# Five more split products in the first up pass, and a new order of the vector work around them

## The chip, the cores and the metric

The kernel runs on one core of one Trainium2 chip. A core has five engines that run side by side and meet only through semaphores: TensorE (PE in the profile, its weight loads are PEld), VectorE (DVE), ScalarE (ACT), GpSimd (POOL) and SyncE (SP), which issues most of the DMAs. Each engine works through its own list of instructions in order; an instruction that waits holds up all that is behind it on its engine.

The metric is the device time of one execution in microseconds (us); the number given for a kernel is the median of its runs.

## What is computed

One transformer layer without its softmax: a linear-attention block and a gated feed-forward block, each behind a layer norm and each added to its input.

```python
# x: 2048 tokens x 1024, 32 heads of 32; F = 3584
q, k, v = split(layernorm(x) @ wqkv)
phi = lambda t: where(t > 0, t + 1, exp(t)) + 1e-6
kv, z = phi(k)^T v, sum(phi(k))            # per head
h = x + (phi(q) kv / (phi(q) z + 1e-6)) @ wo
n = layernorm(h)
out = h + (relu(n @ W_gate) * (n @ W_up)) @ W_down
```

The change lies in the feed-forward block, in the products with `W_gate` and `W_up` of the first half of the tokens.

## The kernel before

**Planning.** The Python code doesn't issue instructions at once. `PL.add(engine, ...)` appends an operation to its engine's list and derives from the buffers that it reads and writes which earlier operations it must wait for. So the order on each engine is the order in which the Python code calls `PL.add`, and nothing reorders it later. Much of the code therefore passes lists of small functions around ("steps"), and calls them at chosen places.

**Two passes.** The feed-forward block handles the tokens in two passes of 1024 (`p_` or `ps_` is 0 and 1; the text calls them pass 1 and pass 2). Each has an up pass (`ffn_unit`, 14 units) and a down pass (`down_pass`, the product with `W_down`). Units come in pairs: an even unit computes the gate for 512 hidden features, the odd one behind it the up product for the same 512. Both write to `hh`, the hidden activations in SBUF; the odd one multiplies its result in.

**Products.** A unit is a matrix product cut in two in each dimension. The kernel uses the Strassen-Winograd scheme, seven block products P1 to P7 in place of eight. Its operands are sums of blocks: `Ssum` of the activations (once a pass), T1 to T4 of the weights (`t_sums`, VectorE, for each unit; T1 and T3 can be one instruction, T13, or apart when `split` is set). A block product is two halves `u`, each of four matmuls with 512 columns.

Some block products are themselves done by the same scheme one level down, as seven small products, each a quarter of the output: P1 of the next unit (R1 to R7, with sums g1 of the weights), and, in the units listed in `M0`, the fifth product P5 (M1 to M7, with sums g5 of T1 that `w_inner` makes, three VectorE instructions). A small product is two matmuls of 256 columns, so a split P5 is 14 of these and a plain one 8 of 512. In a unit outside `M0`, ScalarE copies P5 from PSUM (s5, twice); in one inside it, ScalarE does M5c, M1c, M6c and M4c and VectorE does s5a.

**PSUM.** Eight banks. Partial results are shared by copying a bank before more is accumulated on it: fk1 (P1 of the next unit, ScalarE, at the end of a unit), fk2 (after P6). P2 of a unit accumulates onto the bank that the fk1 before it has read.

**One unit inside `M0`** runs on TensorE as M1, M5, P2, M6, M2, P6 first half, M7, M3, R1, R5, P6 second half, P7 first half, R2, R6, M4, P7 second half, P3 first half, R7, R3, P3 second half, P4 first half, R4, P4 second half. The results leave PSUM as h11 (copy or relu on ScalarE), c22 (VectorE, after P7), Ra (VectorE, for R), c12 (VectorE, after P3), and h21 (in the next unit, `late21`: a copy h21c on ScalarE and for odd units a product on VectorE). An odd unit ends with h2, a VectorE product over two blocks. h21c writes the buffer of c22, which h2 reads.

**What else VectorE does in pass 1's up pass.** For the down pass's weights: WT1, WT2, WT3 (`wd_pair`, from `wraw`, in even units) and WL (`wl_sums`, in odd ones). Sums of the hidden activations for the down pass: D1 (two feature blocks added) and D3 (two token blocks subtracted), made by `hh_pair` in units 3, 5 and 7 for the pairs 0 to 5 of `hh` (`QD = 6`), the rest in the down pass.

**ScalarE** has the layer norm of the tokens of pass 2 as well: 8 tiles `t`, each in three steps (mean, square, norm), handed to `ffn_unit` as `lna` and `lnb`, two in a unit and three in units listed in `LN3`. `ln_o` is their order. A step's small arithmetic is on GpSimd. The norm step stores its tile to DRAM and loads the tile two further on into `hl`.

**The places that matter** in a unit's Python order: `pre` (ahead of all), `wina`, `winb` (after P6), `mid` (GpSimd's sums), `lna`, `lnb`, `tail` (after c12), `later`, `late21`. In `M0` units of pass 1, `lna` stands behind c22, in others behind the first h11. DMAs go to SyncE in the same order: WT3's stores, the weights of a later unit (`load_w_next`), `load_wraw`, the norm's store.

The lines that a reader of the trace meets: L902 all matmuls, L907 ScalarE's copies, L942 and L1586 the LN steps, L1642 and L1647 T1 to T4 and T13, L1697 g1 (from RWG) and g5 (from RO), L1786 VectorE's c22, c12, h11, h21, h2, Ra and s5a, L1798 the relus h22 and h12, L826 WT, L853 WL, L1663 D1, L1668 D3, L1674 D2, L1996 the down pass's sums, L2060 its evacuations.

Of the kernel before, what the change touches and what calls it, by code (L numbers as in the profile page):

```python
# [132 lines left out]
def bass_sequential_preLN__linear_attn_block__glu_gated_reglu__prompt_kernel(  # L133
# [71 lines left out]
    with es:  # L205
# [1522 lines left out]

        late21 = []

        M0 = (2, 4, 6, 8, 10, 12, 13)
        QD = 6
        LN3 = (11,)

        def inner1(ps_, n):
            return 0 < n < NPAIR
# [1 line left out]
        def ffn_unit(ps_, n, pre, wina, winb, mid=(), lna=(), lnb=(), tail=(), tail2=()):  # L1738
# [23 lines left out]
            def go(fs):  # L1762
                for f_ in fs:
                    f_()
# [35 lines left out]
            def out11(u):  # L1800
                if up:
                    ident_act(c12[:, u, :], bank(BA[u]), [B_bank[BA[u]]], [B_c12[u]], "h11c")
                else:
                    d = H2(0, 0)
                    ident_act(d[0][:, u], bank(BA[u]), [B_bank[BA[u]]], d[1][u:u + 1], "h11", func=ACTF.Relu)
# [66 lines left out]
            def p6(u):  # L1872
                prod(u, BB[u], t_blk(u, 1), s_blk(1), False, "P6")
                fk2(u)
# [14 lines left out]
            if not useM:  # L1889
                if plain:  # L1890
                    p1()
                go(late21)
                late21.clear()
                p5(0)
                p2()
                run(mid, 1)
                out11(0)
                go(lna)
                p5(1)
                go(wina)  # L1900
                p6(0)
                r15()
                p6(1)
                run(mid, 1)
            else:
                sub(cX, B_X, B_(0, 0), A(0, 0), True, "M1")
                sub(cD, B_X, G(0), XS(0), False, "M5")
                ident_act(m5, cD, [B_X], [B_s5[0]], "M5c")
                ident_act(c0, cX, [B_X], [B_0], "M1c")
                go(late21)  # L1910
                late21.clear()
                if n == 0:
                    p1()
                else:
                    p2()
                sub(cX, B_X, G(1), XS(1), False, "M6")
                sub(c0, B_0, B_(1, 0), A(0, 1), False, "M2")
                ident_act(cD, cX, [], [B_X], "M6c")
                if n == 0:
                    p2()  # L1920
                go(wina[:1] if m_first else wina)
                out11(0)
                p6(0)
                sub(cX, B_X, G(2), XS(2), False, "M7")
                sub(cD, B_X, B_(1, 1), XS(3), False, "M3")
                dve(ftmp[:, 1, :].rearrange("p (t c) -> p t c", t=2), bank(BE[1]).rearrange("p (t c) -> p t c", t=2),
                    m5.unsqueeze(1).to_broadcast([P, 2, SHB]), [B_X, B_s5[0]], [B_s5[1]], "s5a")
                go(wina[1:] if m_first else ())
                run(mid, 1)
                r15()  # L1930
                p6(1)
                if nxt and ps_:
                    m4()
# [10 lines left out]
            later.clear()  # L1944
            prod(1, BB[1], t_blk(1, 2), s_blk(2), False, "P7")
            run(mid, 3 if m_first else 1)
            evac5(1, 1, BB, c22, B_c22, "c22")
            if m_first:
                go(lna)
            if up:  # L1950
                d, db = H2(0, 0)
                dve(d, d, c12, B_c12, db, "h11", ALU.mult)
            if not up:
                fin5(1, 1, c22, B_c22, "h22")
            prod(0, BC_[0], w_blk(0, 1, 1), s_blk(3), False, "P3")
# [86 lines left out]
        def down_pass(ps_, fill):  # L2042
# [260 lines left out]
            sg5 = l2_sums(q_d1, sgs[4], "sg5")  # L2303
            if not last:
                claim(B_sgg, B_w[0:4])
                at(0, 4, lambda: d1_sum(QD, NPAIR), lambda: d2_sum(QD, NPAIR))
                at(2, 0, *sg6[0:2])
                at(2, 1, *sg6[2:4])
                at(2, 2, lambda: d3_sum(QD, NPAIR), *sg7[0:2])
                at(2, 3, *sg7[2:4])  # L2310
                at(2, 4, *sg4)
                at(1, 1, lambda: d4(0, NH))
                at(1, 5, lambda: d4(NH, NPAIR))
                for i in range(4):
                    at(3, 2 + i, sg5[i])
            else:
                for i in range(4):
                    at(1, 2 + i, sg7[i])
                claim(B_W, B_hnT)
                sg2 = l2_sums(q_10, sgs[2], "sg2")  # L2320

                D4C = ((0, 4), (4, 7), (7, 11), (11, NPAIR))

                def spread(pi, fs, cs=(3, 4, 5, 6)):
                    for f_, c_ in zip(fs, cs):
                        at(pi, c_, f_)
                spread(0, sg2)
                at(0, 6, lambda: d2_sum(0, NH))
                at(2, 0, lambda: d2_sum(NH, NPAIR))
                spread(2, sg6)  # L2330
                spread(3, sg5, (2, 4, 5, 6))
                for i, c_ in enumerate(((1, 6), (3, 3), (4, 6), (5, 0))):
                    at(*c_, sg4[i])
                for i, c_ in enumerate(((1, 4), (1, 6), (3, 5), (5, 0))):
                    at(*c_, lambda i=i: d4(*D4C[i]))
                at(2, 3, lambda: ld_h(0, 1))
                at(3, 6, *each(add_h, U, 0, 1, order=hi))
# [312 lines left out]
        late_load(0)  # L2650
        late_load(1)
        ln_steps = [late_steps(t) for t in range(TPP)]
        ln_o = [(0, 0), (0, 1), (0, 2), (1, 0)]
        for t in range(1, TPP - 1):
            ln_o += [(t, 1), (t + 1, 0), (t, 2)] if t % 2 else [(t, 1), (t, 2), (t + 1, 0)]
        ln_o += [(TPP - 1, 1), (TPP - 1, 2)]
        ln_q += [(ln_steps[t][i], t if i == 2 else None) for t, i in ln_o]

        early = []
        for p_ in range(NPASS):  # L2660
            done = []
            for q in range(NPAIR):
                pre, wina, winb = [], [], []
                if q == 0:
                    pre += x_inner(p_)
                else:
                    pre.append(tq[1])
                if inner1(p_, q + 1):
                    pre += w_inner1(p_, q + 1)
# [4 lines left out]
                if p_ == 0:  # L2674
# [19 lines left out]
                    if q % 2 == 0:  # L2694
                        wds = wd_pair(q)
                        (tail if q == 0 else wina).extend(wds[0:2])
                        if q == 0 or q not in M0:
                            (winb if q else tail).append(wds[2])
                        wls, raw, nxt_raw, raw_l = wl_sums(q // 2)
                        if q == 0:  # L2700
                            raw = [int, int] + [lambda i=i, r=raw: (r[i](), r[i + 1]()) for i in (0, 2)]
                    else:
                        wina += wls
                        raw = raw_l
                        nxt_raw()
                        if q == NPAIR - 1:
                            for _ in range(2):
                                load_wd_next()
# [7 lines left out]
                        tail += [lambda t=t: early_c(t) for t in range(STB)]  # L2716
                    if q + 1 in M0:
                        tail = w_inner(q + 1) + tail
                    if q and q % 2 == 0 and q in M0:
                        tail.append(wds[2])  # L2720
                    if q + 2 == min(M0):
# [44 lines left out]
                        load_wd_next()  # L2766
            if p_ == 0:
                claim([B_D2], B_S)
                d2_sum(0, QD)
            for f_ in late21:  # L2770
                f_()
            late21.clear()
# [94 lines left out]
```

## Time and profile before

| | us |
|---|---|
| median of 3 runs | 709.62 (709.57 to 709.85) |
| the profiled execution, its own time | 709.65 |
| its span, first to last instruction | 707.9 |
| TensorE busy in the span | 702.4 |
| VectorE busy | 613.9 |
| ScalarE busy | 412.5 |
| GpSimd busy | 182.1 |
| pass 1, units 1 to 13 | 236.48 to 388.11 |
| pass 1, down pass, starts | 388.11 |
| pass 2, units 1 to 13 | 479.35 to 629.79 |
| an even unit of pass 1 / an odd one, 1 to 11 | 11.69 / 11.89 |

The granted TensorE clock was 1.000 over the span. A line of a timeline has the start in us from the beginning of the span, the length, engine, source line, operation, what it writes and reads, shape and count; in square brackets is how long the engine sat idle before it and what ended that. Instructions of one engine overlap a little, so lengths add up to more than the distance of starts; times worked out in the text go by starts. Matmul lengths include the pipeline's drain, and the starts are what counts. Now and then a matmul's record is missing.

### The profile page before, as it was taken

The numbers are of one execution on the slowest core, as the hardware profiler recorded it, in microseconds if no ns is written. First come the engines' busy times: TensorE is split into PE (matmuls) and PEld (weight loads), VectorE is DVE, ScalarE is ACT, GpSimd is POOL, SyncE is SP. The second block draws the span as 40 slices with busy tenths as digits, with TensorE's granted clock in tenths as the row PEclk, the third lists the DMA queues.
The fourth block names the chain that finished last, engine by engine and source line by source line (L and its number), as shares of the span: only waits on it lengthen the run. The fifth ranks groups of instructions, "written<-read, shape, count | busy, mean of one in ns | idle before, by whom it ended". The sixth has DMA issues, their size and how long they took to land.

```text
span 707.9 us, 13556 instructions
## 1 busy us (share of the span) xinstructions
PE 702.4 (99%) x5125; PEld 400.6 (57%) x5125; DVE 613.9 (87%) x982; ACT 412.5 (58%) x752; POOL 182.1 (26%) x246
## 2 busy tenths in 40 slices
PE   8999999999999999999999999999999999999998
PEld 3444444444444555555555478865555555568887
DVE  6988867899898999999889968887889888989996
ACT  4887666764863687788788111146666767651010
POOL 3221100114892244334341020321111111001331
PEclk9999999999999999999999999999999999999999
DMA  9852345114998788979997999998555564369996
GB/s 297 262 124 63 38 124 163 37 31 94 225 233 249 228 262 280 288 220 272 307 269 238 304 281 329 319 239 238 148 142 170 146 176 145 109 238 308 348 284 184
DMA packets 170385, 148.80 MB, mean 210 GB/s; under 512 B 54352, under 2 KB 146896, under 8 KB 170320
## 3 DMA queue, kind: packets, MB, share of 16 engines
q1 hardware_dynamic: 165328, 143.35, 68.0%
q0 software_dynamic: 4032, 3.67, 3.6%
q8 instruction: 40, 0.66, 0.4%
q10 hardware_dynamic: 960, 0.92, 0.4%
q14 instruction: 25, 0.20, 0.1%
HBM read 101.97 MB, written 33.88 MB: 192 GB/s over the span
## 4 chain that ended last, share of the span: by engine, by line
PE 89%; ACT 2%; POOL 1%; DVE 1%; issue 1%; DMA 0%; DVEq 0%; POOLq 0%; SPq 0%; ACTq 0%
PE ps L902 89%; ACT RAB L942 1%; POOL RAB L1444 1%; DVE RXH L1526 1%; ACT RAB L1559 1%; DMA RE<-RE 0%; ACT RXH L942 0%; POOL s L966 0%; DVE RAB L989 0%; DVE rden L1384 0%; ACT ps L907 0%; POOL s L948 0%; POOL s L1543 0%; POOL s L963 0%; ACT RX L982 0%
## 5 line engine op out<-in xcount | busy, mean ns | idle before, releaser
L907 ACT ACTIVATE ps<-ps 128x512 f32<-128x512 f32 (+1 forms) x283 | 141.9, 511 | 184.0 <-PE ps L902 140.4
L902 PE MATMUL ps<-RC,RO 128*128 128x512 f16 (+1 forms) x588 | 138.5, 364 | 0.0
L902 PEld LDWEIGHTS ps<-RC,RO 128*128 128x128 f16 x588 | 57.4, 98 | 45.8
L902 PE MATMUL ps<-RC,RWG 128*128 128x512 f16 x320 | 81.1, 380 | 0.2 <-ACT ps L907 0.2
L907 ACT ACTIVATE RE<-ps 128x512 f32<-128x512 f32 (+3 forms) x106 | 63.5, 613 | 29.5 <-PE ps L902 15.2
L902 PE MATMUL ps<-RH,RWG 128*128 128x512 bf16 (+1 forms) x344 | 76.6, 347 | 0.0
L1786 DVE TENSOR_TENSOR RE<-ps,RE 128x1024 bf16<-128x1024 f32 (+1 forms) x49 | 48.6, 993 | 27.4 <-PE ps L902 26.6
L902 PE MATMUL ps<-RH,RO 128*128 128x512 bf16 (+1 forms) x256 | 65.5, 380 | 0.0
L902 PE MATMUL ps<-RW,RAB 128*128 128x256 f16 (+3 forms) x358 | 52.8, 300 | 0.0
L902 PEld LDWEIGHTS ps<-RH,RWG 128*128 128x128 bf16 x344 | 33.1, 98 | 32.4
L902 PE MATMUL ps<-RAB 128*128 128x512 bf16 (+3 forms) x242 | 51.2, 349 | 0.0
L2069 POOL DMA_DIRECT2D out_dram<-RX x20 | 17.9, 1292 | 127.3 <-DVE RX L2060 86.5
L902 PEld LDWEIGHTS ps<-RC,RWG 128*128 128x128 bf16 (+1 forms) x320 | 30.0, 98 | 33.7 <-ACT ps L907 5.1
L804 POOL TENSOR_TENSOR RW<-RW 128x256 f16<-128x256 bf16 x28 | 18.9, 675 | 113.0 <-PE ps L902 70.3
L902 PEld LDWEIGHTS ps<-RW,RAB 128*128 128x128 f16 (+1 forms) x358 | 34.9, 98 | 14.2 <-DVE RXH L1480 0.5
L2060 DVE TENSOR_TENSOR RE<-ps,RE 128x512 f32<-128x512 f32 x46 | 31.6, 687 | 11.4 <-PE ps L902 11.0
L1798 ACT ACTIVATE RAB<-RAB 128x1024 bf16<-128x1024 bf16 x28 | 29.5, 1052 | 16.1 <-DVE RAB L1786 16.1
L902 PEld LDWEIGHTS ps<-RH,RO 128*128 128x128 f16 (+1 forms) x256 | 24.4, 98 | 24.4 <-ACT RX L907 1.5
L1786 DVE TENSOR_TENSOR RAB<-ps,RE 128x1024 bf16<-128x1024 f32 x28 | 34.3, 1223 | 3.8 <-PE ps L902 3.7
L907 ACT ACTIVATE RAB<-ps 128x512 bf16<-128x512 f32 (+2 forms) x55 | 35.9, 654 | 2.0 <-PE ps L902 2.0
L1642 DVE TENSOR_TENSOR RO<-RWG,RO 128x1024 f16<-128x1024 bf16 x54 | 37.0, 685 | 0.0
L1786 DVE TENSOR_TENSOR RAB<-RAB,RE 128x1024 bf16<-128x1024 bf16 (+1 forms) x43 | 36.3, 846 | 0.7
(221 smaller groups left out, 1377.2 us busy)
## 6 DMA issues: line engine op xcount, KB each, us to landing
RWG<-in_B_W_gate_dram SPq DMA_DIRECT2D x28, 512.0 KB, 5.7
RWG<-in_B_W_up_dram SPq DMA_DIRECT2D x28, 512.0 KB, 5.4
RW<-l_scr SPq DMA_DIRECT2D x21, 448.0 KB, 4.9
RE<-l_scr SPq DMA_DIRECT2D x17, 448.0 KB, 4.2
RW<-in_B_W_down_dram SPq DMA_DIRECT2D x14, 512.0 KB, 6.4
l_scr<-RX SPq DMA_DIRECT2D x7, 1024.0 KB, 7.0
RW<-t_scr SPq DMA_DIRECT2D x13, 448.0 KB, 5.8
RE<-in_A_x_dram SPq DMA_DIRECT2D x19, 256.0 KB, 3.6
```

Source lines behind the costliest of these rows:

```text
L804: PL.add("pool", lambda e: e.tensor_tensor(out=ly[:, j, :], in0=x[0], in1=y[0], op=ALU.subtract), deps=[PL.prog["pe"][-1]], reads=x[1] + y ...
L902: lambda e: e.matmul(out_ap, lhsT, rhs, start=start, stop=stop, skip_group_check=skip),
L907: PL.add("act", lambda e: e.activation(out=dst, in_=src, func=func), reads=reads, writes=writes, name=name)
L942: PL.add("act", lambda e: e.activation(out=junk[:, c0:c1], in_=src[:, c0:c1], func=func, scale=scale, accum_out=sv[:, col:col + 1]), reads ...
L1444: PL.add(eng, lambda e: e.tensor_tensor(out=s(i)[0], in0=x[0], in1=y[0], op=op), reads=x[1] + y[1], writes=[B_So[z][i]], name="So%d_%d" % ...
L1526: PL.add("dve", lambda e: e.tensor_tensor(out=hsb[:, hs, :], in0=ps[:, b:b + 2, :], in1=x2(st).rearrange("p (a c) -> p a c", a=2), op=ALU. ...
L1559: PL.add("act", lambda e: e.activation(out=xo[:, kx, :], in_=hsb[:, hs, :], func=ACTF.Identity, bias=s2[:, ks, 4:5], scale=s2[:, ks, 2:3]) ...
L1642: PL.add(eng, lambda e: e.tensor_tensor(out=tb(j)[0](r), in0=x[0](r), in1=y[0](r), op=ALU.subtract), reads=rd, writes=bt(j, r), name="T%d_ ...
L1786: PL.add("dve", lambda e: e.tensor_tensor(out=dst, in0=in0, in1=in1, op=op), reads=reads, writes=writes, name=name)
L1798: PL.add("act", lambda e: e.activation(out=d, in_=d, func=ACTF.Relu), reads=[], writes=db, name=name)
L2060: PL.add(eng, lambda e: e.tensor_tensor(out=dst, in0=in0, in1=in1, op=op), reads=reads, writes=writes, name=name)
L2069: PL.add("pool", lambda e: e.dma_start(dst, src, accum_op=ALU.add), reads=[bsrc], writes=[B_hscr[st]], slot=sl, name="acc_%d_%d" % (st, dh))
```

## The change

- `M0` becomes all units from 2 on: the units 3, 5, 7, 9 and 11 of pass 1 get the split fifth product too. With it they get g5 sums for themselves (in the tail of the even unit before), T1 and T3 apart for the unit behind them, `lna` behind c22, and one idle place at the head of `mid`.
- `QD` becomes 0: `hh_pair` isn't called in pass 1 any more. D1 and D3 of the pairs 0 to 5 are made in its down pass: D1 at the start, ahead of D2, and D3 ahead of the rest of D3.
- In the even units 2 to 12 (`T2E`), T2 of the unit moves from its own `pre` to the tail of the odd unit before, ahead of h2; the odd unit's h21 (copy and product) moves from behind M1c to behind the first h11, and so behind WT1.
- In units that aren't `M0` units of pass 1, so in all of pass 2, h11 stands ahead of c22 on VectorE instead of behind it.
- The LN steps come in a new order, and the unit with three of them is unit 1 instead of 11.

```diff
-        M0 = (2, 4, 6, 8, 10, 12, 13)
-        QD = 6
-        LN3 = (11,)
+        M0 = tuple(range(2, NPAIR))
+        QD = 0
+        QE = 6
+        LN3 = (1,)
+        T2E = (2, 4, 6, 8, 10, 12)
...
                 ident_act(c0, cX, [B_X], [B_0], "M1c")
-                go(late21)
-                late21.clear()
+                if not (m_first and n in T2E):
+                    go(late21)
+                    late21.clear()
...
                 out11(0)
+                go(late21)
+                late21.clear()
                 p6(0)
...
             run(mid, 3 if m_first else 1)
+            h11 = []
+            if up:
+                d11, db11 = H2(0, 0)
+                h11.append(lambda: dve(d11, d11, c12, B_c12, db11, "h11", ALU.mult))
+            if not m_first:
+                go(h11)
             evac5(1, 1, BB, c22, B_c22, "c22")
             if m_first:
                 go(lna)
-            if up:
-                d, db = H2(0, 0)
-                dve(d, d, c12, B_c12, db, "h11", ALU.mult)
+                go(h11)
...
-                at(0, 4, lambda: d1_sum(QD, NPAIR), lambda: d2_sum(QD, NPAIR))
+                at(0, 4, lambda: d1_sum(QE, NPAIR), lambda: d2_sum(QE, NPAIR))
...
-                at(2, 2, lambda: d3_sum(QD, NPAIR), *sg7[0:2])
+                at(2, 2, lambda: d3_sum(QD, QE), lambda: d3_sum(QE, NPAIR), *sg7[0:2])
...
-        ln_o = [(0, 0), (0, 1), (0, 2), (1, 0)]
-        for t in range(1, TPP - 1):
-            ln_o += [(t, 1), (t + 1, 0), (t, 2)] if t % 2 else [(t, 1), (t, 2), (t + 1, 0)]
-        ln_o += [(TPP - 1, 1), (TPP - 1, 2)]
+        ln_o = [(0, 0), (0, 1), (1, 0), (0, 2), (1, 1), (1, 2), (2, 0), (2, 1), (3, 0), (2, 2), (3, 1), (3, 2), (4, 0),
+                (4, 1), (5, 0), (4, 2), (5, 1), (5, 2), (6, 0), (6, 1), (7, 0), (6, 2), (7, 1), (7, 2)]
...
-                else:
+                elif p_ or q not in T2E:
                     pre.append(tq[1])
...
-                        raw = raw_l
+                        raw = [int] * (q in M0) + raw_l
...
+                    if q + 1 in T2E:
+                        tail.append(tq[1])
...
-                d2_sum(0, QD)
+                d1_sum(QD, QE)
+                d2_sum(0, QE)
```

## The prediction

> **What bounds the kernel now.** I read the page's busy shares first, then the chain that ended last in order of time, then busy time by stretches (one stretch per unit of pass 1's up pass), then VectorE's, ScalarE's and SyncE's timelines inside two units.
>
> ```profile
> PE 702.4 (99%) x5125; PEld 400.6 (57%) x5125; DVE 613.9 (87%) x982; ACT 412.5 (58%) x752; POOL 182.1 (26%) x246
> ```
>
> ```profile
> 207.52 474.52 PE ps L902 x3025
> 682.04 0.00 issue
> 682.04 23.10 PE ps L902 x210
> ```
>
> TensorE is the bound: from 207.52 to 705.14 us the chain is its matmuls and nothing else. By their starts, a 512-wide matmul is followed by the next after 0.216 us and a 256-wide one after 0.109, and from 222 us on only three gaps exceed this, 0.13 to 0.17 us each. So removed matmuls are worth their full time, and no wait stands there to be removed. What can go wrong is a new wait.
>
> ```profile
> 248.37:260.06 11.69, 11.69 (x70) 6.59 (x69) 11.10 (x19) 10.20 (x19) 5.71 (x7) 1.00 0.91 292
> 260.06:271.94 11.88, 11.88 (x63) 6.06 (x62) 10.89 (x17) 9.05 (x18) 6.98 (x7) 1.00 0.86 271
> 271.94:283.63 11.69, 11.69 (x69) 6.59 (x68) 11.12 (x19) 10.20 (x19) 4.13 (x6) 1.00 0.76 238
> 330.79:342.68 11.89, 11.89 (x64) 6.06 (x62) 9.61 (x15) 9.06 (x18) 5.66 (x7) 1.00 0.90 242
> ```
>
> These are units 2, 3, 4 and 9 (columns: length, then busy time of PE, PEld, DVE, ACT, POOL). An even unit, with its fifth product split, takes 11.69 us, an odd one 11.89. VectorE is idle 0.6 us in an even unit, 1.0 in unit 3 and 2.3 in unit 9: it is the second bound.
>
> ```profile
> 268.11 1.22 DVE L1786 TENSOR_TENSOR RE<-ps,RE 128x1024 bf16<-128x1024 f32 x1 [0.79 <-PE ps L902]
> 270.45 1.21 DVE L1786 TENSOR_TENSOR RE<-ps,RE 128x1024 bf16<-128x1024 f32 x1
> 271.58 0.44 DVE L1697 TENSOR_TENSOR RE<-RO 128x512 f16<-128x512 f16 x1
> 272.05 0.62 DVE L1697 TENSOR_TENSOR RE<-RO,RE 128x256 f16<-128x256 f16 x2
> 272.59 1.22 DVE L1786 TENSOR_TENSOR RAB<-RAB,RE 128x2048 bf16<-128x2048 bf16 x1
> 273.72 0.68 DVE L1642 TENSOR_TENSOR RO<-RWG,RO 128x1024 f16<-128x1024 bf16 x1
> ...
> 277.12 0.68 DVE L1786 TENSOR_TENSOR RE<-ps,RE 128x512 f32<-128x512 f32 x1
> ...
> 278.92 0.69 DVE L1642 TENSOR_TENSOR RO<-RWG 128x1024 f16<-128x1024 bf16 x1
> 279.78 1.23 DVE L1786 TENSOR_TENSOR RAB<-ps,RE 128x1024 bf16<-128x1024 f32 x1 [0.18 <-PE ps L902]
> ```
>
> VectorE from the end of unit 3 through unit 4: c22 of the odd unit, c12, the three g5 sums, h2, T2, later s5a, T1, then c22 of the even unit. Between the first c22 and the last it never idles; its spare time is 0.79 us ahead of the odd unit's c22 (2.11 in unit 9) and 0.18 ahead of the even one's. A 1024-wide sum holds it 0.60 us from start to start.
>
> **The products.** Each of units 3, 5, 7, 9, 11 loses eight 512-wide matmuls and gains fourteen 256-wide ones: 8 x 0.216 = 1.73 against 14 x 0.109 = 1.53. The stretches say the same: 11.887 - 11.690 = 0.197. Times five: **-0.985 us**.
>
> The Trainium skill, "TensorE: Matmul & The Clock Gate", Back-to-back issue gap, speaks against this: in a stream of weight loads and matmuls it has one matmul per 81 ns at 128 columns and per 131 ns at 512. A line through these gives, as an estimate, 98 ns at 256, and 14 x 98 against 8 x 131 would make each unit 0.32 us longer, 711.2 us in all. The trace disagrees, with 216 ns at 512 columns.
>
> **VectorE's new work in an odd unit.** g5 for it (three sums, 271.58 to 272.59: 1.01), s5a (0.60), and T1 and T3 apart for the next unit (2 x 0.60, for one T13 of 1.14): +1.67. Units 3, 5, 7 lose a D1 and a D3 sum (two 1024-wide, 262.31 to 263.64: 1.33). Net +0.34 there and +1.67 in 9 and 11, in units 0.20 shorter, against idle pairs of 1.57 and 2.86 us. It fits in sum, with about 1 us left per pair; where the pieces stand decides.
>
> *Odd unit.* g5 now stands ahead of T3 and WT3 in the even unit's tail, so T2 of the odd unit ends 2.3 us after the unit's start and its P6 begins at 2.60: hidden. VectorE reaches c22 about 0.9 us before P7 is over: hidden. ScalarE takes M5c, M1c, M6c, M4c for two s5 copies, and the LN step that stood behind h11 now stands behind c22 with the other; the queue then ends about 10.9 us into the unit, and fk1 waits for c12 until 11.4: hidden by 0.5.
>
> *Even unit.* From the odd c22 on nothing is idle, so the one sum that is new in this stretch, T3, makes all behind it 0.60 late. T2 ahead of h2 keeps T2 early (it ends 1.9 us into the unit; P6 begins at 2.60; unmoved and with T3 ahead it would end at 3.1). h21c, behind h2 in ScalarE's queue, now also stands behind M6c and h11; fk2, queued behind it, ends 4.9 us into the unit and P7 begins at 5.19: hidden by 0.2 after the hand-over. Two waits open:
> - s5a ended at 277.80, M4 (same bank) began at 278.44. It will end at 278.40; VectorE's end to the matmul it releases is 0.05 to the weight load and 0.05 more (g5 ends 272.02, load 272.07; load 272.33, matmul 272.38). M4 is 0.06 late.
> - c22 starts 0.34 late (0.60 less the idle time). h22, one LN step and fk1 follow it on ScalarE without a gap; fk1 ended at 283.73 and will end at 284.07, so P2 of the odd unit starts at 284.17 and not at 283.63 + 0.44. 0.10 late, the 0.06 included.
> Four pairs (4/5 to 10/11) at 0.10 and unit 12 at 0.06 (no LN step stands in its queue): **+0.45**. Ends: 0 if the chain is 0.1 shorter, and 1.35 if each pair pays 0.3, half of the added 0.60.
>
> **SyncE.** WT3 ends 1.0 us later in the odd unit, and its stores, two weight loads and the next wraw loads are queued behind it. Weights are needed a unit later. wraw is closer: it landed 3.6, 3.5 and 2.9 us before WT1 needed it in units 4, 6, 8, but 1.0 in unit 10 (345.72 against 346.71; a transposing load of 1.86 us stands in that queue) and 1.7 in unit 12. With 1.0 later stores and a unit 0.2 shorter, WT1 of unit 10 waits about 0.2: **+0.2**, all of which the chain passes on. Ends: 0 and 0.5. In unit 2, where no T3 is new, WT1 starts 0.6 earlier (h21 now follows it), just as its wraw lands (251.79): 0, s5a there has 0.6 to spare.
>
> **The LN steps.** Norms 1, 3, 5 move a unit earlier, with their stores and the loads of hl; each load is still issued at least a unit before its mean step (loads land in 2.6 to 7.7 us). The third step of unit 1 is 1.14 us in 2.1 us of ScalarE's idle time: 0. GpSimd does the same sums and is idle 4 us and more per unit. Without that cover a step costs its excess once.
>
> **The sums in the down pass.** D1 and D3 of pairs 0 to 5 are two 3072-wide sums of 1.75 (the D2 of that size, 389.26), 3.5 to 3.6 us with gaps.
>
> ```profile
> 410.59 1.09 DVE L1996 TENSOR_TENSOR RWG<-RAB,RWG 128x1792 f16<-128x1792 bf16 x1
> 415.61 1.42 DVE L2060 TENSOR_TENSOR RE<-ps,RE 128x512 f32<-128x512 f32 x2 [3.93 <-PE ps L902]
> ```
>
> VectorE idles 3.93 us there, after the last of the sums that follow; D2 and sg6 end near 402.6 and TensorE reads them from 412.28 on. 0. With that cover gone, the first evacuation would be late by the excess, and its bank is next written near 434: still 0.
>
> **h11 ahead of c22** (pass 2; unit 1 of pass 1). In pass 2 c22 idles 0.14 ahead of itself at 510.58; with h11 (0.60) in front it starts 0.4 later and ends at about 9.45 us into the unit, and P4, which needs it, begins at 9.75: hidden by 0.2. 0; ends 0 and 7 x 0.1.
>
> **Sum.** -0.985 + 0.45 + 0.2 = -0.33 on the profiled execution's own 709.65 us (span 707.9 and 1.7 around it), 0.03 over the median, 709.62: **709.3**.
>
> **Rivals.**
> - *No new wait* (the chain 0.1 shorter, wraw in time): 709.65 - 0.985 = 708.6. For it: all margins are near zero, not far below. Chance 0.25.
> - *Waits use up the gain*: 0.3 per pair, 1.35, and 0.5 for wraw: 710.2; from 709.7 to 711.0. Against it: idle time of 1 us per pair remains. 0.16.
> - *Slower*: ScalarE's queue in odd units. Both LN steps now stand between M4c and fk1 with 0.5 us to spare. If a step waits there (GpSimd's lsum sum of 1.15 us can stand ahead of a rstd), all beyond 0.5 delays P2 of the next unit. It passes 711.0 from about 0.9 us of waiting in each of five units; at 1.15 it is 709.3 + 5 x 0.65 = 712.5. Against it: each norm follows its square step by half a unit or more. 0.13.
> - *Narrow matmuls don't pay*: if the 0.098 us weight load did not hide beside a 256-wide matmul, spacing would be 0.207, and five units 5 x (14 x 0.207 - 1.73) = +5.8: 715.5. The even units' 11.69 speak against it. The Trainium skill's rule named above belongs here. 0.02.
> - *Faster by more*: all five savings and the three present gaps (0.46): 708.2. Nothing in the change touches those. 0.03.
>
> **How the numbers follow.** My forecast has 0.41 (709.0 to 709.7). The range 708.4 to 710.6 takes in no wait, the forecast and most of the used-up gain, 0.8 in all. 0.2% is 1.4 us, about what a measurement of this kernel can tell from no change: slower 0.13 + 0.02, faster 0.03, within 0.82.
>
> **What would show it.** Odd units 3 to 11 of 70 matmuls and 11.69 to 11.8 us; gaps of some 0.05 us ahead of M4 in units 4 to 12 and ahead of the first P2 in 5 to 11; WT1 of unit 10 waiting for wraw; VectorE's idle time ahead of the first down-pass evacuation down from 3.93 to about 0.3. It is wrong if fk1 in odd units waits for an LN step, if a unit is above 11.89, or if pass 2's units leave 11.69.

## The result

The changed kernel takes 713.32 us, the median of 6 runs (712.38 to 713.96), against 709.82 (709.57 to 710.04) for 6 runs of the kernel before. The ratio is 1.0047, with a 95% interval of 1.0034 to 1.0060: half a per cent slower, and 2.7 us above the range that was forecast. The profiled execution, the slowest of the six, took 713.96 us, with a span of 712.2.

### The profile after

From the page of the changed kernel, the busy times and the chain that ended last, by engine:

```profile
PE 703.0 (99%) x5155; PEld 404.3 (57%) x5155; DVE 623.8 (88%) x1003; ACT 414.1 (58%) x762; POOL 177.8 (25%) x246
...
PE 76%; DVE 9%; DMA 3%; ACT 2%; issue 2%; POOL 1%; SPq 1%; DVEq 0%; POOLq 0%; ACTq 0%
```

TensorE's busy time hardly moves, but the chain is no longer its own: TensorE has 76% of it, against 89% on the page of the kernel before, and VectorE 9% against 1%. Busy time by units of pass 1 (units 2, 3, 4, 8, 9; columns: length, then busy time of PE, PEld, DVE, ACT, POOL):

```profile
249.38:261.74 12.36, 11.86 (x69) 6.57 (x68) 11.28 (x18) 9.70 (x19) 6.60 (x8) 1.00 0.88 276
261.74:273.43 11.69, 11.69 (x69) 6.66 (x68) 10.55 (x18) 9.82 (x19) 4.84 (x6) 1.00 0.79 235
273.43:285.61 12.18, 11.86 (x69) 6.54 (x68) 11.94 (x20) 9.69 (x20) 5.23 (x9) 1.00 0.81 267
...
321.18:333.98 12.80, 12.04 (x69) 6.50 (x68) 12.56 (x20) 9.87 (x19) 4.70 (x7) 1.00 0.93 269
333.98:345.67 11.69, 11.69 (x69) 6.64 (x68) 10.55 (x18) 9.82 (x19) 4.83 (x6) 1.00 0.79 210
```

The odd units took the whole saving: 11.89 to 11.69 each. The even units pay: 11.69 became 12.36, 12.18, 12.19, 12.80, 12.41 and 12.18 in units 2 to 12, 3.99 us in sum. Units 2 to 12 together took 129.58 us before and take 132.58 now. The rest of the 4.3 us between the two spans is 1.01 us ahead of unit 1 and 0.23 in one unit of pass 2. The stretch from the start of pass 1's down pass to unit 1 of pass 2 has its 91.24 us as before.

In the even units TensorE waits at one place, M4 (and in unit 8 at M5 too). TensorE in unit 4 (timeline; R6 is `ps<-RX,RAB`, M4 is `ps<-RC,RE`; in brackets the wait that the profile sees):

```profile
279.71 0.38 PE L902 MATMUL ps<-RX,RAB 128*128 128x256 f16 x2
280.41 0.39 PE L902 MATMUL ps<-RC,RE 128*128 128x256 f16 x2 [0.32 <-DVE RE L1788]
```

Two 256-wide matmuls after 279.71, M4 was due at 279.93; it came 0.48 later, behind s5a. What VectorE and GpSimd did just before, in two timelines of the changed kernel (L1788 is what was L1786; WT1, h21, s5a; and GpSimd's first WM sum of the unit, which a matmul releases):

```profile
277.46 1.23 DVE L826 TENSOR_TENSOR RW<-RW 128x2048 f16<-128x2048 bf16 x1
278.60 1.16 DVE L1788 TENSOR_TENSOR RAB<-RAB,RE 128x1024 bf16<-128x1024 bf16 x1
279.68 0.68 DVE L1788 TENSOR_TENSOR RE<-ps,RE 128x512 f32<-128x512 f32 x1
```

```profile
277.64 1.57 POOL L879 TENSOR_TENSOR RAB<-RW 128x256 f16<-128x256 bf16 x1 [4.00 <-PE ps L902]
```

h21 takes 1.16 us; in the kernel before, where it stood ahead of WT1, the same product took 0.69 (h21, WT1):

```profile
275.38 0.69 DVE L1786 TENSOR_TENSOR RAB<-RAB,RE 128x1024 bf16<-128x1024 bf16 x1
275.98 1.22 DVE L826 TENSOR_TENSOR RW<-RW 128x2048 f16<-128x2048 bf16 x1
```

And GpSimd's sum takes 1.57 where its like takes 0.67 (at 283.39 of this profile). The two fit together: the sum came while WT1 ran and ended 0.52 after WT1's end (279.21 against 278.69), and h21 ended 0.55 after the sum. Both are a little under what each needs by itself (0.67, and 0.60 from start to start). So first WT1 holds the sum up, and then the sum, next in turn, holds h21 up. In the kernel before the same sum was stretched in the same way (here its line), but what VectorE ran after WT1 was s5a, which has one input in PSUM, and that took 0.68 as ever:

```profile
276.15 1.58 POOL L879 TENSOR_TENSOR RAB<-RW 128x256 f16<-128x256 bf16 x1 [4.04 <-issue]
```

The Trainium skill, "SBUF — State Buffer", Who interferes with whom, states the rule that this follows: a VectorE instruction with both inputs in SBUF and a GpSimd instruction that reads SBUF share one read interface, whichever comes first holds it for its whole instruction, and the other blocks; a VectorE instruction with at most one SBUF input, outside the modes that use both ports, does not contend. The rows above agree, with 0.48 us as the price here. The part on the cores has the engines meet only through semaphores; here two of them meet without one, since h21 waits for no semaphore of GpSimd and is held all the same.

Two more places of the same kind. In unit 8, GpSimd's 128x512 sum WL starts behind three small LN instructions, and VectorE's first sum of g5, which takes 0.42 elsewhere, takes 1.04; M5 is 0.50 late. GpSimd first, then VectorE:

```profile
319.24 0.19 POOL L963 TENSOR_TENSOR s<-s 128x1 f32<-128x1 f32 x1 [0.71 <-ACT RE L942]
319.51 0.57 POOL L966 TENSOR_TENSOR s<-s,neghalf 128x1 f32<-128x1 f32 x1
320.18 0.27 POOL L1581 TENSOR_SCALAR s<-s 128x1 f32<-128x1 f32 x1
320.40 1.15 POOL L869 TENSOR_TENSOR RX<-RW,RX 128x512 f16<-128x512 f16 x1
```

```profile
319.67 1.22 DVE L1788 TENSOR_TENSOR RE<-ps,RE 128x1024 bf16<-128x1024 f32 x1
320.80 1.04 DVE L1697 TENSOR_TENSOR RE<-RO 128x512 f16<-128x512 f16 x1
```

In units 2 and 10, last, WT1 waits for wraw (VectorE's timeline, the wait in brackets); in unit 10 it then takes 1.45 in place of 1.23, since a WM sum has begun at 349.88:

```profile
253.58 1.23 DVE L826 TENSOR_TENSOR RW<-RW 128x2048 f16<-128x2048 bf16 x1 [0.87 <-DMA RW<-in_B_W_down_dram]
254.72 1.16 DVE L1788 TENSOR_TENSOR RAB<-RAB,RE 128x1024 bf16<-128x1024 bf16 x1
...
350.18 1.45 DVE L826 TENSOR_TENSOR RW<-RW 128x2048 f16<-128x2048 bf16 x1 [0.42 <-DMA RW<-in_B_W_down_dram]
```

### The profile page after: what moved, and what is told of

The parts are those of the page before. It is cut to its first block, busy times and chain, and to the rows that moved or that the text cites. A ratio compares the mean times of both kernels' runs of the same rounds, so it can differ in the third digit from the quotient of the medians.

```text
span 712.2 us, 13655 instructions
## 1 busy us (share of the span) xinstructions
PE 703.0 (99%) x5155; PEld 404.3 (57%) x5155; DVE 623.8 (88%) x1003; ACT 414.1 (58%) x762; POOL 177.8 (25%) x246
## 4 chain that ended last, share of the span: by engine, by line
PE 76%; DVE 9%; DMA 3%; ACT 2%; issue 2%; POOL 1%; SPq 1%; DVEq 0%; POOLq 0%; ACTq 0%
PE ps L902 76%; DVE RAB L1788 2%; DMA RW<-in_B_W_down_dram 2%; DVE RE L1788 2%; DVE RW L826 2%; ACT RAB L942 1%; SPq L653 1%; DVE RO L1642 1%; DVE RE L1697 1%; POOL RAB L1444 1%; DMA r_scr<-RW 1%; DVE RXH L1526 1%; ACT RAB L1559 1%; DMA RE<-RE 0%; DVE RAB L1697 0%
## 5 line engine op out<-in xcount | busy, mean ns | idle before, releaser
L907 ACT ACTIVATE ps<-ps 128x512 f32<-128x512 f32 (+1 forms) x293 | 144.9, 505 | 182.7 <-PE ps L902 147.7
L902 PE MATMUL ps<-RC,RO 128*128 128x512 f16 (+1 forms) x568 | 132.1, 360 | 0.0
L902 PEld LDWEIGHTS ps<-RC,RO 128*128 128x128 f16 x568 | 55.6, 98 | 41.2 <-ACT ps L907 1.0
L1788 DVE TENSOR_TENSOR RE<-ps,RE 128x1024 bf16<-128x1024 f32 (+1 forms) x54 | 52.1, 964 | 25.2 <-PE ps L902 25.2
L1788 DVE TENSOR_TENSOR RAB<-RAB,RE 128x1024 bf16<-128x1024 bf16 (+1 forms) x43 | 38.7, 901 | 0.7
L902 PE MATMUL ps<-RE 128*32 128x33 bf16 (+1 forms) x668 | 35.4, 203 | 0.3 <-DVE RE L1697 0.3
```

The lines of the kernel that those rows point to most:

```text
L902: lambda e: e.matmul(out_ap, lhsT, rhs, start=start, stop=stop, skip_group_check=skip),
L907: PL.add("act", lambda e: e.activation(out=dst, in_=src, func=func), reads=reads, writes=writes, name=name)
L1788: PL.add("dve", lambda e: e.tensor_tensor(out=dst, in0=in0, in1=in1, op=op), reads=reads, writes=writes, name=name)
```

## The experiments

Theory A: GpSimd's sums hold up VectorE's sums that read SBUF twice, above all h21 behind WT1; that is what costs. Theory B: h21 is slow by its place or its operands, or VectorE simply has too much to do. Theory C: ScalarE's queue is too long with the new products (the slower rival of the prediction).

The table puts all profiles side by side: units 2 to 12 of pass 1 in sum, the start of unit 1, and the profiled execution's own time less that start. 128.59 is eleven times 11.69, the whole saving.

| kernel | units 2-12 | unit 1 at | time less start | median of runs | ratio (95%) |
|---|---|---|---|---|---|
| before | 129.58 | 236.48 | 473.17 | 709.82 | |
| changed | 132.58 | 237.49 | 476.47 | 713.32 | 1.0047 (1.0034 to 1.0060) |
| e1 WM behind P7 | 130.03 | 236.26 | 473.72 | 710.32 | 1.0012 (1.0002 to 1.0021) |
| e2 h21 behind s5a | 129.16 | 237.11 | 473.01 | 710.26 | 1.0007 (0.9998 to 1.0017) |
| e3 old units | 129.58 | 236.34 | 473.53 | 709.87 | 1.0005 (0.9996 to 1.0015) |
| e4 h11 back | 132.27 | 237.00 | 476.18 | 712.35 | 1.0040 (1.0025 to 1.0055) |
| e5 e2, old LN order | 130.07 | 236.79 | 473.69 | 710.48 | 1.0010 (1.0001 to 1.0019) |
| e6 products alone | 132.27 | 236.59 | 475.86 | 712.81 | 1.0038 (1.0024 to 1.0051) |
| e7 e5, WY later | 130.07 | 236.07 | 473.78 | 710.87 | 1.0013 (1.0004 to 1.0021) |
| e8 WM twice | 131.70 | 236.54 | 475.36 | 711.90 (one run) | |
| e9 e2, LN steps swapped | 128.59 | 235.97 | 472.43 | 709.37 | 0.9995 (0.9987 to 1.0004) |
| e10 e9, WY later | 128.59 | 237.70 | 472.29 | 709.83 | 0.9998 (0.9985 to 1.0012) |
| e11 as e9 | 128.59 | 236.11 | 472.45 | 709.85 | 1.0002 (0.9993 to 1.0011) |
| e12 as before | 129.58 | 236.23 | 473.18 | 709.41 (one run) | |

The kernel before had medians of 709.50 to 709.68 beside e1 to e12.

### e1: GpSimd's first WM sum behind P7

```diff
                             raw = [int, int] + [lambda i=i, r=raw: (r[i](), r[i + 1]()) for i in (0, 2)]
+                        else:
+                            raw = [int] + raw
```

> In the even units of pass 1 GpSimd's first raw sum of W (WM) is moved behind product P7 and the others follow it, so that none is queued behind WT1. Theory A (the two engines stand in each other's way): h21 takes 0.68 us again in units 4, 6, 8 and 12 (1.16 in the changed kernel), s5a ends 0.47 earlier there, M4 waits under 0.1 us in units 4, 6 and 12 (0.48 in the changed kernel); units 2 and 10, where WT1 waits for a DMA, keep a part of their 0.66 and 0.71. The time falls by some 4 x 0.45 = 1.8 us from 713.3, to 711.5; less if the moved sums are in the way of another VectorE sum. Theory B (h21 is slow by its place or its operands, whatever GpSimd does): h21 still takes 1.16 us, M4 is still 0.48 late, 713.3. Theory C (ScalarE's queue is too long with the new products): M4 is late as before, and the wait is put down to ScalarE; 713.3.

h21 takes 0.68 in every even unit, and M4 of units 2, 4, 6 and 12 waits for less than 0.05 us. VectorE in unit 4, in the same order as in the changed kernel:

```profile
275.56 1.23 DVE L826 TENSOR_TENSOR RW<-RW 128x2048 f16<-128x2048 bf16 x1
276.70 0.68 DVE L1788 TENSOR_TENSOR RAB<-RAB,RE 128x1024 bf16<-128x1024 bf16 x1
277.30 0.68 DVE L1788 TENSOR_TENSOR RE<-ps,RE 128x512 f32<-128x512 f32 x1
```

Nothing on VectorE or ScalarE was changed, so B and C fall for this wait. The up pass is 2.55 us shorter than in the changed kernel, more than the 1.8 expected, since unit 2 gains all of its 0.67. What stays: M5 and M4 of unit 8 (0.51 and 0.13), 0.10 in units 5 and 11, where the moved sums now stretch a sum of g5 from 0.29 to 0.64, and M4 of unit 10, 0.49 late with h21 at 0.68: there WT1 waits 0.41 for wraw (a load that scatters, as told below).

### e2: h21 behind s5a

```diff
-                go(late21)
+                l21 = list(late21)
                 late21.clear()
+                for f_ in l21:
+                    f_(0)          # the copy h21c
                 p6(0)
...
+                for f_ in l21:
+                    f_(1)          # the product h21
                 go(wina[1:] if m_first else ())
```

> VectorE's product h21 is moved behind the sum s5a in the even units of pass 1 (its copy on ScalarE stays where it is), all else as in the changed kernel. Theory A: after WT1 comes s5a, which reads PSUM; GpSimd's first WM sum runs beside it, as before the change, h21 takes 0.68 us, s5a ends 1.16 us earlier than in the changed kernel, M4 waits for nothing in units 4, 6, 8 and 12; 713.3 - 4 x 0.48 = 711.4, or lower where units 2 and 10 gain too (WT1's end 0.7 us earlier than needed): 710.5. What comes behind s5a is 0.68 later than without h21, so M7's and c22's readers could wait. Theory B: s5a is early too, so M4 doesn't tell; but h21 still takes 1.16 us in its new place, or s5a is the one that gets long. Theory C: M4 still late, behind ScalarE.

The other way out: GpSimd stays, VectorE gives way. By the up pass it is the better one (129.16 against 130.03 in e1); the medians, 710.26 and 710.32, don't tell the two apart. GpSimd's sum and VectorE's WT1, s5a and h21 in unit 4:

```profile
276.58 1.58 POOL L879 TENSOR_TENSOR RAB<-RW 128x256 f16<-128x256 bf16 x1 [4.00 <-PE ps L902]
```

```profile
276.40 1.23 DVE L826 TENSOR_TENSOR RW<-RW 128x2048 f16<-128x2048 bf16 x1
277.55 0.68 DVE L1788 TENSOR_TENSOR RE<-ps,RE 128x512 f32<-128x512 f32 x1
278.15 0.68 DVE L1788 TENSOR_TENSOR RAB<-RAB,RE 128x1024 bf16<-128x1024 bf16 x1
```

The same stretched sum now lies under s5a, which reads PSUM and isn't held; h21 has its 0.68 back. s5a writes SBUF as h21 does, so it is what they read that makes the difference. No M4 waits in any unit. In pass 1 only M5 of unit 8 is left (0.51), with 0.06 behind it. So the product that the change put behind WT1 was harmless one place further on.

### e3: the old units, all else as in the changed kernel

```diff
-        M0 = tuple(range(2, NPAIR))
+        M0 = (2, 4, 6, 8, 10, 12, 13)
```

> Units 3, 5, 7, 9, 11 lose the inner fifth product again (8 matmuls 512 wide instead of 14 of 256); the places of h21, T2, the D sums and the LN steps stay as in the changed kernel. The matmuls cost 5 x 0.197 = 0.985 us more again. Theory A: GpSimd still holds up h21 (1.16 us in even units), but VectorE is some 0.6 us earlier in the even unit without T3's sums, so M4 is at most 0.1 late: 713.3 + 0.985 - 3.9 + 0.3 = 710.7. Theory C (the new order is what costs, the products nothing): the stalls stay at 0.48 a unit, 714.2. If h21 takes 0.68 here, the new products are what puts it beside the GpSimd sum.

h21 is held up here too, 1.16 in all six even units from 2 on (VectorE in unit 4):

```profile
275.07 1.23 DVE L826 TENSOR_TENSOR RW<-RW 128x2048 f16<-128x2048 bf16 x1
276.21 1.16 DVE L1788 TENSOR_TENSOR RAB<-RAB,RE 128x1024 bf16<-128x1024 bf16 x1
277.30 0.68 DVE L1788 TENSOR_TENSOR RE<-ps,RE 128x512 f32<-128x512 f32 x1
```

But without T3's sum s5a ends at 277.98, 6.18 into the unit, and M4 is due at 6.50: no unit waits, and all have the lengths of the kernel before. The new order costs nothing that shows by itself (0.25 us in the medians, with an interval that holds 1); the collision is paid for only where the products have used up the slack. It came out 0.8 under the expectation, which had left 0.3 of stalls and the late start in.

### e4: h11 behind c22 again

```diff
-            if not m_first:
-                go(h11)
             evac5(1, 1, BB, c22, B_c22, "c22")
             if m_first:
                 go(lna)
-                go(h11)
+            go(h11)
```

> In pass 2 the product h11 goes behind the evacuation c22 again, all else as in the changed kernel. If h11 ahead of c22 is what makes P4 wait 0.22 us in one unit of pass 2, that gap goes and the time is 713.1; if GpSimd's sum beside WX1 and T4 is the cause alone, the gap shrinks by less than that but goes as well, since c22 is then 0.5 us earlier. Pass 1 is as in the changed kernel (even units 12.18 us, h21 1.16 us). The start of unit 1, 1.0 us later in the changed kernel's profile than in the kernel before, differs between these runs if it belongs to the start-up's transfers, and is 1.0 us late in all four if it belongs to the change.

A miss: the wait of P4 in pass 2 stays (0.22), so h11's place doesn't make it. In that unit c22 is late because GpSimd's sums of Y stand beside T4 and WX1. In the changed kernel T4 takes 1.00 where it takes 0.71 in the kernel before, and WX1 takes 0.90 where it takes 0.42 in other units, having come just after a GpSimd sum began at 596.40. VectorE:

```profile
596.45 0.90 DVE L775 TENSOR_TENSOR RW<-RW 128x512 f16<-128x512 bf16 x1
597.27 1.21 DVE L1788 TENSOR_TENSOR RAB<-ps,RE 128x1024 bf16<-128x1024 f32 x1
```

The first of these GpSimd sums starts 4.2 us into the unit in the profiles of before, e1 and e3, where P4 doesn't wait, and at 4.5 in those of the changed kernel, e2 and e4, where it does. What moves it stays open. The expectations of e7 and e10 call it a load's landing, but no run shows that: in all of these profiles GpSimd's wait ahead of the sum, for TensorE and a transfer, ends 4.11 us into the unit, and the store that the sum itself waits for has landed before the unit begins. The start of unit 1 differs among the four runs, 236.26 to 237.11: it isn't a fixed 1.0 us late.

### e5: e2 with the LN steps in the old order

```diff
-        LN3 = (1,)
+        LN3 = (11,)
...
-        ln_o = [(0, 0), (0, 1), (1, 0), (0, 2), ...
+        ln_o = [(0, 0), (0, 1), (0, 2), (1, 0)]
+        for t in range(1, TPP - 1):
+            ln_o += [(t, 1), (t + 1, 0), (t, 2)] if t % 2 else [(t, 1), (t, 2), (t + 1, 0)]
+        ln_o += [(TPP - 1, 1), (TPP - 1, 2)]
```

> h21 behind s5a as in e2, and the LayerNorm steps back in the old order (ln_o as before the change, LN3 = (11,)). In e2 the up pass of pass 1 loses only 0.51 us, all of it ahead of M5 of unit 8, where VectorE's first sum of g5 takes 1.05 us instead of 0.42 while GpSimd runs a 128x512 sum (WL) that starts behind three small LN instructions. Theory A: with the old order GpSimd is not behind that sum at that moment, g5 takes 0.42, the gap goes, units 3 to 12 are all 11.69 us, the up pass is 0.985 us shorter than before the change and the time is 709.6 - 0.98 = 708.6 (708.9 where pass 2's P4 waits 0.22 us again). Rival: the gap in unit 8 has nothing to do with the LN order (the T5 chain of that unit is simply late): it stays at 0.51, 709.1. Second rival: the old order's steps fall onto another sum and a gap opens elsewhere.

The second rival. M5 of unit 8 is in time, but now M5 of units 4 and 10 is 0.50 late, each behind a g5 sum of 1.04 beside the same WL sum, and P2 of unit 12 waits 0.34 for fk1 (three LN steps stand in unit 11's ScalarE queue in this order). GpSimd at the end of unit 3:

```profile
270.13 0.20 POOL L963 TENSOR_TENSOR s<-s 128x1 f32<-128x1 f32 x1 [0.71 <-ACT RE L942]
270.40 0.56 POOL L966 TENSOR_TENSOR s<-s,neghalf 128x1 f32<-128x1 f32 x1
271.06 0.27 POOL L1581 TENSOR_SCALAR s<-s 128x1 f32<-128x1 f32 x1
271.29 1.15 POOL L869 TENSOR_TENSOR RX<-RW,RX 128x512 f16<-128x512 f16 x1
```

The pattern is that of unit 7 in the changed kernel. In the old order units 3 and 9 have a square step (t, 1) as their first LN step, in the new one unit 7 alone. So the LN order isn't free, and by the up pass (130.07 against 129.16 in e2) the change's new order is the better of the two; the medians, 710.48 and 710.26, don't show it.

### e6: the products alone, in the kernel before

```diff
-        M0 = (2, 4, 6, 8, 10, 12, 13)
+        M0 = tuple(range(2, NPAIR))
```

> The kernel before with the inner fifth product in units 3, 5, 7, 9, 11 too, and nothing else of the change (h21 at its old place ahead of WT1, D sums in the up pass, old LN order). Theory A: h21 is not behind WT1, so GpSimd's sum runs under s5a as before and h21 takes 0.68; M4 is at most 0.1 late. VectorE has 1.56 us idle per pair of units before, the products ask for 1.67 more, so in the units that keep a D pair (3, 5, 7) it runs 0.1 to 0.7 us late by the end: stalls of 0.1 to 0.5 us in units 4 to 8, none later. The time is 709.6 - 0.98 + 0.3 to 1.5 = 708.9 to 710.1. Rival (VectorE's lateness is what the products cost, wherever h21 stands): even units lose 0.48 or more each, 711.5 to 713.

Here the rival's time came true, 711.5 to 713, and theory A's 708.9 to 710.1 was a miss. h21, ahead of WT1, takes 0.69, and M4 is never late, as A has it. But units 4 to 12 still lose 0.50 to 0.76 in every even one. In units 4 to 10 most of it is at P6, which starts 0.49 to 0.54 late behind T2; in unit 12 the larger part is P2, 0.34 behind fk1 as in e5. VectorE's h2 and T2, then TensorE, in unit 4:

```profile
273.46 1.22 DVE L1786 TENSOR_TENSOR RAB<-RAB,RE 128x2048 bf16<-128x2048 bf16 x1
274.60 0.68 DVE L1642 TENSOR_TENSOR RO<-RWG,RO 128x1024 f16<-128x1024 bf16 x1
```

```profile
274.58 0.38 PE L902 MATMUL ps<-RC,RO 128*128 128x256 f16 x2
275.34 0.60 PE L902 MATMUL ps<-RC,RO 128*128 128x512 f16 x2 [0.37 <-DVE RO L1642]
```

This is the wait that T2 ahead of h2 removes. So the products need a new order on VectorE, the change has it, and one step of it, h21 behind WT1, gives the gain back by another door.

### e7 and e10: the last sums of Y one product later

```diff
-                    wys = [f_ for m in range(NM) for f_ in y_wsums(m) + [int]]
+                    wys = [f_ for m in range(NM) for f_ in ([int] + y_wsums(m) if m == 6 else y_wsums(m) + [int])]
```

> As e5, and in pass 2 GpSimd's last group of sums of Y starts one product later, so that its first one no longer falls beside T4 and WX1 in unit 10. Theory A: P4 of that unit waits for nothing, whatever the load's landing; 708.6, and 0.2 less than e5 wherever e5's profile has that gap. Rival: the gap comes back at another product of the same or the next unit, since VectorE's sums with two SBUF inputs stand everywhere there; same as e5.

> As e9, with the last group of Y's sums of pass 2 on GpSimd one product later (as in e7). Theory A: up pass as in e9; unit 10 of pass 2 is 11.69 us whatever the landing of its load, 708.6. Rival: no gain over e9, since that wait comes in some executions only, or a new wait in units 10 and 11 of pass 2.

P4 of pass 2 waits in neither (e9 and e11, without this, have it: their unit takes 11.92, so 0.23 is lost in each; the 0.45 in the expectation of e11 is the distance over a missing matmul record). In e5, though, it is gone as well, and in the medians nothing shows. Inconclusive as a gain.

### e8: the WM sum twice

```diff
-            raw = [lambda: addw(0, wr(0, 1), wr(0, 0)),
+            raw = [lambda: [addw(0, wr(0, 1), wr(0, 0)) for _ in range(2 if m else 1)],
```

> The changed kernel with GpSimd's first WM sum of each even unit from 2 on issued twice (the same values are written again), so that two GpSimd sums of 0.67 us stand in a row behind WT1. If GpSimd and VectorE take turns, h21 gets in behind the first one: it takes 1.16 us as in the changed kernel, M4 waits 0.48, and the second sum ends late. If GpSimd keeps the port while it has work, h21 takes 1.16 + 0.67 = 1.83 us and M4 waits 1.15. If GpSimd has nothing to do with it, M4 waits 0.48 and neither sum is stretched.

They take turns. M4 of units 4, 6, 10 and 12 waits 0.48 to 0.49, as that of 4, 6 and 12 does in the changed kernel; the two GpSimd sums, VectorE's WT1 and h21 in unit 4:

```profile
276.01 2.65 POOL L879 TENSOR_TENSOR RAB<-RW 128x256 f16<-128x256 bf16 x2 [4.00 <-PE ps L902]
```

```profile
275.84 1.23 DVE L826 TENSOR_TENSOR RW<-RW 128x2048 f16<-128x2048 bf16 x1
276.98 1.16 DVE L1788 TENSOR_TENSOR RAB<-RAB,RE 128x1024 bf16<-128x1024 bf16 x1
```

The second sum, issued at 277.67, took 0.99 and ended at 278.66, 0.52 after h21: GpSimd's second sum waited for h21, not h21 for it. In this run h21 is held by one GpSimd sum and not by two.

### e9 and e11: e2 with two LN steps swapped

```diff
-                (4, 1), (5, 0), (4, 2), (5, 1), (5, 2), (6, 0), (6, 1), (7, 0), (6, 2), (7, 1), (7, 2)]
+                (5, 0), (4, 1), (4, 2), (5, 1), (5, 2), (6, 0), (6, 1), (7, 0), (6, 2), (7, 1), (7, 2)]
```

> As e2 (h21 behind s5a), and in the new LN order the two steps of unit 7 change places: (5, 0) first, (4, 1) second. In the changed kernel and in e2 unit 7 is the only odd unit whose first LN step is a second one (t, 1), and the only one with a slow g5; in e5 those were units 3 and 9, and the slow g5 stood there: a step (t, 1) in the first place of an odd unit puts three small GpSimd instructions ahead of the 128x512 sum WL, which then runs beside g5. Theory A: with the swap no odd unit has it, g5 takes 0.42 us everywhere, M5 of unit 8 waits for nothing, units 2 to 12 are all 11.69 us, and pass 1's up pass is 0.985 us shorter than before the change: 709.6 - 0.98 = 708.6, 0.23 more where P4 of pass 2 waits. Rival: the step falls onto another sum in its new place; a gap of 0.3 to 0.5 us stays in unit 7 or 8, 709.1.

> The kernel of e9, unchanged, once more. Its first profile had units 2 to 12 all at 11.69 us and a span of 706.7, 1.2 under the kernel before, and yet its median was only 0.13 lower. If the rest is lost ahead of pass 1 (unit 1 has begun between 235.97 and 237.70 us in the profiles so far, of kernels whose code is the same up to there), units 2 to 12 are 11.69 us again, whatever the time, and the time less the start of unit 1 is that of the first profile, but for up to 0.45 of pass 2's P4. If it is lost in the up pass (wraw's landing, another sum beside GpSimd's), a unit longer than 11.69 us shows it.

> The kernel before, once more, for a second profile of it. Unit 1 began at 236.48 us in the first. If that start scatters over 1.7 us in any kernel, another value is likely here and the time moves with it; if it is steadier without the new products, it stays within some 0.2 us of 236.48 and the time within 0.2 of 709.65.

In the up pass of pass 1 theory A holds to the last wait. Busy time in units 2, 3, 4, 8 and 9 of e9:

```profile
247.86:259.55 11.69, 11.64 (x69) 6.64 (x68) 10.96 (x18) 9.90 (x19) 5.70 (x9) 1.00 0.90 285
259.55:271.24 11.69, 11.64 (x69) 6.64 (x68) 10.55 (x18) 9.72 (x19) 4.32 (x5) 1.00 0.79 236
271.24:282.93 11.69, 11.64 (x69) 6.61 (x68) 11.45 (x20) 9.57 (x20) 5.23 (x9) 1.00 0.84 277
318.00:329.69 11.69, 11.64 (x69) 6.62 (x68) 11.45 (x20) 9.67 (x19) 5.10 (x7) 1.00 1.05 297
329.69:341.38 11.69, 11.64 (x69) 6.62 (x68) 10.54 (x18) 9.84 (x19) 4.83 (x6) 1.00 0.80 214
```

Every unit has 11.69, three profiles agree (e9, e10, e11), and the up pass is 0.99 shorter than before the change, the whole of the term that the prediction gave the products. From unit 1 on these profiles are 0.72 to 0.89 us shorter than the two of the kernel before (472.29 to 472.45 against 473.17 and 473.18).

The medians don't show it: 709.37 and 709.85, with intervals that hold 1. The runs of e9 and e11 scatter from 708.35 to 710.92, most of the kernel before's beside them lie between 709.1 and 710.1. The profiled execution was among the fastest of each. What the profiles show of the scatter lies ahead of unit 1, where VectorE, ScalarE, GpSimd and SyncE run the same instructions in the same order in e9 as in the kernel before: unit 1 starts at 235.97 to 237.70 in the profiles with the changed order, at 236.48 and 236.23 in the two of the kernel before. (e12 lies 0.25 us and its time 0.24 below the first, just outside the 0.2 that its expectation has for a steady start.) In e10, the latest, GpSimd's first L1444 sum waits 1.13 for a DMA (0.22 in e9):

```profile
195.29 1.16 POOL L1444 TENSOR_TENSOR RAB<-RE 128x512 f16<-128x512 bf16 x1 [1.13 <-DMA RE<-RE]
```

In the changed kernel's own profile the 1.01 arises near 8.5 us, at a load of `wqkv`. Whether these loads land later more often in the new kernels, and why, stays open: two profiles of the kernel before are too few to say. e9 is thus no slower than the kernel before and faster in its fastest runs, but not faster by a median that could be told.

## Why the prediction was wrong

- **The products: right.** Five times 0.197 was forecast and measured to the hundredth. That narrow matmuls don't pay was rightly given a small chance: 70 matmuls make 11.69. The Trainium skill's 81 ns per matmul at 128 columns and 131 at 512 ("TensorE: Matmul & The Clock Gate", Back-to-back issue gap) don't hold in this trace, which has 0.216 us at 512.
- **"VectorE's new work", its part "Even unit": the step that failed.** The order and the place of each piece were right: by that sum h21 was to start where s5a had started, at 277.12 or 5.18 us into unit 4, and it started at 5.17. Then the step gave h21 the length, 0.68, that it had in a place where GpSimd was idle. It was 1.16, s5a ended 6.93 into the unit and not 6.46, and M4 was 0.48 late where 0.06 had been forecast. The term of +0.45, with an upper end of 1.35, measured 3.99 with SyncE's term and the LN steps' in it: 0.49 to 0.50 each in units 4, 6 and 12 from h21 alone, 1.11 in unit 8 (M5 0.50, M4 0.60), 0.72 in unit 10 (wraw, and a WT1 that is held itself; h21 takes 0.68 there) and 0.67 in unit 2. e1 and e2 take the collision away from either side, and M4's wait goes with it. With h21 at 0.68 in its new place (e1), M4 of unit 4 is 0.02 late, near the 0.06 of the forecast. P2 of the odd units, the other wait of that step, never came, and not only because M4's delay makes room for fk1. In e9 no M4 waits, c22 of unit 4 starts 8.17 us into the unit (8.18 by the forecast), and yet the first half of fk1 ends 0.31 us into unit 5 and not 0.44, in time for P2: this chain was priced 0.1 too long.
- **"GpSimd does the same sums and is idle 4 us and more per unit": the same fault** in the LN steps. Idle time on GpSimd was beside the point; when its sums run decides which VectorE sum they hold. This is M5's 0.50 in unit 8, and e9 takes it away.
- **SyncE: right in kind, wrong to give it one size.** WT1 of unit 10 waits for wraw, 0.42 where 0.2 was forecast; in e1, where nothing else is in the way, that makes M4 0.49 late. But the same wait is missing in e2, e4, e8 and e9, whose orders on SyncE are the same: the landing scatters. In unit 2 it is 0.87 here, 0.62 in e4, and none in e1, e2, e8 and e9. The "0.6 to spare" of that unit was real: in e8 h21 is held there too, wraw is in time, and M4 isn't late. Both together make its 0.67.
- **The down-pass sums: right.** VectorE's idle time ahead of the first evacuation went from 3.93 to 0.31:

```profile
419.62 1.42 DVE L2069 TENSOR_TENSOR RE<-ps,RE 128x512 f32<-128x512 f32 x2 [0.31 <-PE ps L902]
```

- **h11 ahead of c22: right**, it costs nothing; the unit of 11.92 in pass 2 has another cause (e4).
- **"Waits use up the gain"**: its own terms, -0.985, 1.35 and 0.5 on 709.65, add up to 710.5 and not to 710.2. The range up to 710.6 still takes that in.
- **The slower rival** had the sign and not the mechanism. In unit 3 ScalarE's queue ends 10.74 us into the unit (10.9 forecast) and fk1 waits for c12 until 11.43 (11.4 forecast). No rival had a VectorE sum that is longer in its new place, so the range missed too, by 2.7 us.

## What to carry to other kernels

Before an elementwise instruction with both inputs in SBUF is moved, look at what GpSimd runs at that time, not at how idle GpSimd is: its length belongs to its place as much as to its shape. A GpSimd sum of 0.67 that was harmless beside an instruction that reads PSUM cost 0.48 beside one that doesn't. Where two such streams must cross, put an instruction that reads PSUM at the crossing, as e2 does. And a change with several parts should be taken apart with the slack in view: here the new order alone cost nothing that shows (e3), the products alone cost 3 us at another place (e6), and the loss of the two together came from a collision that the new order had already made and that its slack had hidden.

## What the runs showed of the hardware

- Taking turns: a GpSimd sum (0.67 alone) that comes while a two-input VectorE sum runs starts to work when that one ends, ahead of VectorE's next, and that next one is then held until it has ended (0.68 becomes 1.16). With two GpSimd sums in a row, VectorE gets in between (e8).
- The wait lies inside the held instruction's length, on both engines: VectorE's h21 has no idle time before it in any view, and the chain of waits names VectorE, not GpSimd. Only the length compared with other instructions of the same shape gives it away.
